# Attention with capped scores and a bilinear feed-forward on one core: a later product with the reciprocals, earlier first weights, and scores in single-pass parts

## The chip, the core and the metric

The kernel runs on one core of a Trainium2 chip. TensorE (PE in the profile) multiplies matrices into PSUM, ScalarE (ACT) evaluates functions and copies, VectorE (DVE) works element by element, GpSimd (POOL) takes what is left over, and SyncE (SP) issues nearly all the DMAs. The metric is the device time of one execution in microseconds (us). The kernel before has a median of 782.43 us over three runs.

## The reference

```python
# q, k, v: [4 batches, 12 heads, 448, 64]; w_a, w_b: [768, 1536]; w_out: [1536, 768]
scores = np.matmul(q, k.transpose(0, 1, 3, 2)) / np.sqrt(64)
scores = cap * np.tanh(scores / cap)
attn = np.exp(scores - scores.max(-1, keepdims=True))
attn = attn / (attn.sum(-1, keepdims=True) + 1e-9)
x = np.matmul(attn, v).transpose(0, 2, 1, 3).reshape(1792, 768)
out = ((x @ w_a) * (x @ w_b)) @ w_out
```

The weights arrive as 64-bit floats, so the kernel has to turn them into 32-bit ones itself; q, k and v are 32-bit.

## The kernel before

**Pairs.** The 48 heads are worked in 24 pairs: two heads of one batch, one on partitions 0 to 63, the other on 64 to 127. For a pair, `load_pair` (L191) issues four DMAs each for k and q and one for v; `prep_pair` (L205) transposes k and q on VectorE (L210). `scores` (L213) makes the transposed scores in four blocks of 128 keys, the last of 64 (448 = 3 x 128 + 64). A block is one matmul for each head, on 64 rows of the array (L223), in full fp32; a short last block takes 64 columns of weights. ScalarE applies tanh (L224) and exp (L225), and VectorE adds the exponentials of the blocks into `psum` (L229, L232, L233). `attend` (L235) multiplies the exponentials with v. Score blocks go through two PSUM buffers of two banks each (`ps_sc`); everything else takes four buffers of one bank (`ps_1`), save that from pair 12 on the product with v and the row sums of a pair take a `ps_sc` buffer together (L237).

**Normalizing.** `normalize` (L250) sums `psum` over its partitions on TensorE with a selecting matrix (L260), takes the reciprocal on VectorE (L268), writes it to DRAM (`rd`, L269) and reads it back spread over 64 partitions for each head (`den`, L273); VectorE multiplies (L274). The result is a part of x. For pairs 0 to 11 (the first 896 tokens) `split_x` (L280) splits it into a high part in fp32r, a format that TensorE takes in a single pass, and the remainder, also fp32r: `xhi` and `xlo`. For pairs 12 to 23 it goes to DRAM and is split later.

**Feed-forward.** `ffn(g)` (L365) works on one half of the tokens. Each product of two split factors is three matmuls: high by high, high by low, low by high (L377 to L379, L408 to L410). A weight tile of 128 x 768 goes through `load64` (L300, the raw 64-bit form, two buffers, SyncE), `ready_w` (L320: two steps on ScalarE, L337 and L338, three on VectorE, L339 to L341, one addition on GpSimd, L342, and a store to DRAM for the second half, L343), and `split_w` (L346).

**Order.** The main loop (L450) runs over pairs and goes through the letters of a string: P prepares the next pair, A and N attend and normalize the previous one, S and T are the first and second two score blocks, F is a share of the feed-forward:

```python
order = "PASNFTF" if pi <= NPG else "SFANPFTF"
```

Pairs 0 to 11 (NPG = 12) have no feed-forward beside them; pairs 12 to 23 run beside `ffn(0)`, and `ffn(1)` follows alone. The first `ready_w` are called at the ends of iterations 8 to 11 (L469). The written order is not the final one: a scheduler that simulates the program's time sets the order of the instructions on each engine, except for those marked with `keep_in_program_order`, as the first raw loads are (L317). On every engine work is then taken in that order, so what stands behind a waiting instruction waits too.

## Time and profile before

| | us |
|---|---|
| median of 3 runs (781.46 to 782.46) | 782.43 |
| profiled execution | 784.88 |
| its span (first to last instruction) | 783.1 |
| TensorE busy in the span | 732.6 (94%) |
| VectorE busy | 424.1 (54%) |
| ScalarE busy | 331.6 (42%) |
| GpSimd busy | 185.4 (24%) |

The span is what the profiler's rows cover; the execution's own time lies 1.8 us above it. Busy time is the union of an engine's instructions, where a matmul's end is modelled. In the rows further down, a bracket such as `[7.69 <-DMA den<-rd]` says that the engine had stood idle for 7.69 us just before, and that a DMA writing `den` from `rd` ended it.

### The profile page before, as it was taken

Reading aid. Unit: us, or ns where it says so; the run is one execution under the profiler, and the core shown is the slowest. Engines: PE = TensorE matmul, PEld = TensorE weight load, DVE = VectorE, ACT = ScalarE, POOL = GpSimd, SP = SyncE. Lnnn points to the kernel's source line nnn. Section 1 sums busy time; section 2 is a strip of 40 time slices with the busy share of each in tenths; the row PEclk is TensorE's granted clock in tenths of the full one; section 3 lists DMA queues with packets and bytes.
Section 4 is the critical chain, followed back from the end, with each engine's and each line's share of the span. In section 5 each row is a group of like instructions: output and inputs, shape, how many; then the busy total and the mean of one; then the engine's idle time right before and its main releaser. Section 6 shows DMA issues by size and latency. Waiting matters only on the chain.

```text
span 783.1 us, 10042 instructions
## 1 busy us (share of the span) xinstructions
PE 732.6 (94%) x3888; PEld 560.7 (72%) x3888; DVE 424.1 (54%) x562; ACT 331.6 (42%) x402; POOL 185.4 (24%) x102
## 2 busy tenths in 40 slices
PE   5699776997899999998999999999999999999996
PEld 1233223675587677775777787999999999999996
DVE  4576789898624876465665654733213342243222
ACT  5588587575655755354651631022232202212110
POOL 0011244364302343025340221002102201200100
PEclk9899989999899999999899999999999999999999
DMA  6455687885643664336442133542102102111002
GB/s 122 92 105 114 164 180 203 243 228 185 192 120 120 184 198 136 96 108 195 143 156 85 41 105 109 184 135 81 41 21 100 41 21 81 62 41 41 1 35 111
DMA packets 151926, 90.47 MB, mean 116 GB/s; under 512 B 114624, under 2 KB 139456, under 8 KB 151872
## 3 DMA queue, kind: packets, MB, share of 16 engines
q1 hardware_dynamic: 151872, 89.77, 40.3%
q8 instruction: 32, 0.52, 0.3%
q14 instruction: 22, 0.18, 0.1%
HBM read 67.24 MB, written 22.50 MB: 115 GB/s over the span
## 4 chain that ended last, share of the span: by engine, by line
PE 61%; DMA 17%; DVE 11%; issue 4%; SPq 3%; ACT 3%; POOL 1%; DVEq 0%; ACTq 0%; POOLq 0%
PE po L408 6%; PE po L410 6%; PE po L409 6%; PE phb L377 6%; PE phb L378 6%; PE phb L379 6%; PE pha L377 6%; PE pha L379 6%; PE pha L378 6%; DMA den<-rd 5%; PE psc L223 4%; DMA rd<-rec 4%; PE pv L245 2%; DMA xl<-xd 2%; DMA w64o<-in_moe_w_out_dram 2%
## 5 line engine op out<-in xcount | busy, mean ns | idle before, releaser
L223 PE MATMUL psc<-tq,tk 64*128 64x448 f32 (+1 forms) x384 | 97.1, 602 | 25.9 <-DVE den L274 12.3
L408 PE MATMUL po<-who,gh 128*128 128x384 f32 x336 | 114.1, 340 | 1.0 <-DVE acc L414 0.8
L409 PE MATMUL po<-wlo,gh 128*128 128x384 f32 x336 | 112.5, 335 | 0.0
L410 PE MATMUL po<-who,gl 128*128 128x384 f32 x336 | 112.5, 335 | 0.0
L377 PE MATMUL phb<-xhi,whb 128*128 128x448 f32 x288 | 108.0, 375 | 0.0
L377 PE MATMUL pha<-xhi,wha 128*128 128x448 f32 x288 | 107.6, 374 | 0.0
L378 PE MATMUL phb<-xlo,whb 128*128 128x448 f32 x288 | 106.9, 371 | 0.0
L379 PE MATMUL phb<-xhi,wlb 128*128 128x448 f32 x288 | 106.6, 370 | 0.0
L379 PE MATMUL pha<-xhi,wla 128*128 128x448 f32 x288 | 106.2, 369 | 0.0
L378 PE MATMUL pha<-xlo,wha 128*128 128x448 f32 x288 | 106.1, 369 | 0.0
L224 ACT ACTIVATE pf<-psc,capt 128x896 f32<-128x896 f32 x96 | 85.1, 909 | 44.3 <-PE psc L223 43.6
L223 PEld LDWEIGHTS psc<-tq,tk 64*128 64x128 f32 (+1 forms) x384 | 29.5, 180 | 68.6 <-issue 35.4
L225 ACT ACTIVATE pf<-pf,capt 128x1792 f32<-128x1792 f32 (+1 forms) x48 | 77.0, 1604 | 1.2
L414 DVE TENSOR_TENSOR acc<-po,acc 128x384 f32<-128x384 f32 x84 | 45.9, 554 | 48.2 <-PE po L410 48.1
L408 PEld LDWEIGHTS po<-who,gh 128*128 128x128 f32 x336 | 63.0, 188 | 8.5 <-issue 3.2
L384 DVE TENSOR_TENSOR asb<-phb,asb 128x448 f32<-128x448 f32 x48 | 29.8, 621 | 68.7 <-PE phb L379 68.6
L245 PE MATMUL pv<-pf,ldv 128*64 128x448 f32 x288 | 63.6, 563 | 2.5 <-ACT pf L225 2.5
L409 PEld LDWEIGHTS po<-wlo,gh 128*128 128x128 f32 x336 | 63.1, 188 | 0.8 <-issue 0.7
L410 PEld LDWEIGHTS po<-who,gl 128*128 128x128 f32 x336 | 63.0, 188 | 0.7 <-issue 0.7
L377 PEld LDWEIGHTS phb<-xhi,whb 128*128 128x128 f32 x288 | 55.0, 191 | 11.9 <-issue 6.1
L377 PEld LDWEIGHTS pha<-xhi,wha 128*128 128x128 f32 x288 | 54.5, 189 | 11.7 <-issue 6.1
L386 DVE TENSOR_TENSOR gl<-asb,gh 128x448 fp32r<-128x448 f32 x48 | 51.0, 1063 | 21.6 <-ACT gh L385 21.4
(73 smaller groups left out, 971.0 us busy)
## 6 DMA issues: line engine op xcount, KB each, us to landing
w64a<-in_moe_w_a_dram SPq DMA_DIRECT2D x12, 768.0 KB
w64b<-in_moe_w_b_dram SPq DMA_DIRECT2D x12, 768.0 KB
w64o<-in_moe_w_out_dram SPq DMA_DIRECT2D x12, 768.0 KB
ldk<-in_k_dram SPq DMA_DIRECT2D x96, 56.0 KB
ldq<-in_q_dram SPq DMA_DIRECT2D x96, 56.0 KB
ldv<-in_v_dram SPq DMA_DIRECT2D x24, 224.0 KB
den<-rd SPq DMA_DIRECT2D x48, 112.0 KB
out_dram<-acc SPq DMA_DIRECT2D x13, 384.0 KB
```

The source lines that it names most:

```text
L223: nc.tensor.matmul(to, tk[o, at : at + (P if n == 2 else R)], tq[o], start=True, stop=True)
L224: nc.scalar.activation(pf[:, 2 * i : 2 * i + n], psc[:, :n, :S], AF.Tanh, scale=capt[:, 1:2])
L225: nc.scalar.activation(pf, pf, AF.Exp, scale=capt[:, 0:1])
L245: nc.tensor.matmul(t[j * D : (j + 1) * D, :S], tv[:, j * (NC3 + 1) + c], p, start=(c == 0), stop=False)
L377: nc.tensor.matmul(t[:, :S], wh[:, kk], xhi[:, kk, cs], start=(kk == 0), stop=False)
L378: nc.tensor.matmul(t[:, :S], wh[:, kk], xlo[:, kk, cs], start=False, stop=False)
L379: nc.tensor.matmul(t[:, :S], wl[:, kk], xhi[:, kk, cs], start=False, stop=(kk == NK - 1))
L386: nc.vector.tensor_sub(gl[:, cs], asb[h], f32(gh[:, cs]))
L408: nc.tensor.matmul(t[:, :HALF], gh[:, cs], wh, start=(f == fs[0]), stop=False)
L409: nc.tensor.matmul(t[:, :HALF], gh[:, cs], wl, start=False, stop=False)
L410: nc.tensor.matmul(t[:, :HALF], gl[:, cs], wh, start=False, stop=(f == fs[-1]))
L414: nc.vector.tensor_add(acc[:, ti, hs], t[:, :HALF], acc[:, ti, hs])
```

## The change

Five edits:

- For pair 0 the four DMAs of q are issued by ScalarE instead of SyncE.
- `normalize` ends with the loads of `den`; the product with it, and the split or store of the result, become a step of its own, `scale`. In iterations up to 12 step M scales the pair before the one just normalized, with the product marked to keep the program's order; after iteration 12 it scales the pair just normalized, later in the iteration than before. Iteration 12 does the last of the first half at its end.
- Two raw weight tiles are loaded at the end of iteration 2, and from iteration 9 on one more is loaded before each conversion. The shifted low words go back into the raw tile, so the separate `wr` buffer is gone. `rec` has one buffer instead of two.
- For pairs from 12 on, transposed q and k are split into a high part (ScalarE, fp32r) and the remainder (VectorE), and a score block is three single-pass products instead of one in fp32. The last block of 64 keys becomes a matmul on all 128 rows, whose weights `kz` hold both heads' last keys in two corners (copied by GpSimd) and zeros elsewhere.
- In iterations 11 and 12 the transposes of the next pair move behind the second score blocks.

```diff
@@ load_pair @@
+                    eng = nc.scalar if nm == "q" and pi == 0 else nc.sync
+                    eng.dma_start(t[rows], cols.rearrange("(c p) d -> p c d", p=BLK))
@@ prep_pair @@
             nc.vector.transpose(tt, t.rearrange("p c d -> p (c d)"))
+            if pi >= NPG:
+                hi = qk.tile([P, S], F32R, tag=f"h{nm}", name=f"h{nm}_{pi}", bufs=1)
+                lo = qk.tile([P, S], F32R, tag=f"t{nm}", name=f"l{nm}_{pi}")
+                nc.scalar.copy(hi, tt)
+                nc.vector.tensor_sub(lo, tt, f32(hi))
+                tt = (hi, lo)
             stk[pi].append(tt)
+        if pi >= NPG:
+            for z, x in zip(kz, stk[pi][0]):
+                for j, o in enumerate(own):
+                    nc.gpsimd.tensor_copy(z[o, j * R : (j + 1) * R], x[o, krem[j] : krem[j] + R])
+
+    products = ((0, 0), (0, 1), (1, 0))
@@ scores, pairs from 12 on @@
+            elif n == 2:
+                for x, y in products:
+                    for j, o in enumerate(own):
+                        kk = tk[x][o, j * R + c * P : j * R + (c + 1) * P]
+                        nc.tensor.matmul(psc[:, j, :S], kk, tq[y][o], start=(x + y == 0), stop=(x == 1))
+            else:
+                for x, y in products:
+                    nc.tensor.matmul(psc[:, 0, :S], kz[x], tq[y], start=(x + y == 0), stop=(x == 1))
@@ normalize @@
-        rec = sm.tile([P, CP], F32, tag="rec", name=f"rec_{pi}")
+        rec = sm.tile([P, CP], F32, tag="rec", name=f"rec_{pi}", bufs=1)
...
-        nc.vector.tensor_mul(den, t[:, :S], den)
+        pvs[pi] = (t, den)
+
+    def scale(pi):
+        g, r = divmod(pi, NPG)
+        t, den = pvs.pop(pi)
+        tc.keep_in_program_order(nc.vector.tensor_mul(den, t[:, :S], den))
         if g == 0:
             split_x(r, den, nc.gpsimd)
@@ ready_w @@
-        lr = wp.tile([P, DM], I32, tag="wr", name=f"wl{nm}_{f}", bufs=1)
-        nc.scalar.activation(lr, lw.bitcast(U32), AF.Copy, scale=2.0**-29)
+        nc.scalar.activation(lw, lw.bitcast(U32), AF.Copy, scale=2.0**-29)
...
-        nc.gpsimd.tensor_tensor(wt, wt, lr, op=ALU.add)
+        nc.gpsimd.tensor_tensor(wt, wt, lw, op=ALU.add)
@@ main loop @@
-            order = "PASNFTF" if pi <= NPG else "SFANPFTF"
+            order = "PASMNFTF" if pi < NPG - 1 else "ASMNFTPF" if pi <= NPG else "SFANFMTPF"
...
+                elif step == "M" and (pi > NPG or pi > 1):
+                    scale(pi - (1 if pi > NPG else 2))
...
+            if pi == 2:
+                load64()
+                load64()
             if NPG - AHEAD <= pi < NPG:
+                if pi > NPG - AHEAD:
+                    load64()
                 ready_w()
...
+            if pi == NPG:
+                scale(pi - 1)
```

**Where the product stands.** VectorE, first part of the program, before: from the last addition of pair 0's exponentials to pair 1's reciprocal. A row has the line, the operation, what it writes and reads (`den_0` is pair 0's, `pf_1_0` pair 1's first exponentials), and its size.

```order
L233 TENSOR_TENSOR psum0_163<-psum0_163,pf_0_1_239 128x896
L268 RECIPROCAL rec_0_297<-sum_0_288 128x112
L229 TENSOR_TENSOR psum1_164<-pf_1_0_265 128x896
L210 STREAM_TRANSPOSE tk_3_319<-ldk_3_276 128x448
L210 STREAM_TRANSPOSE tq_3_321<-ldq_3_281 128x448
L274 TENSOR_TENSOR den_0_300<-pv_0_256,den_0_300 128x448
L232 SCALAR_TENSOR_TENSOR psum1_164<-pf_1_1_306,capt_133,psum1_164 64x448 x2
L283 CAST xhi_165<-den_0_300 128x448
L233 TENSOR_TENSOR psum1_164<-psum1_164,pf_1_1_306 128x896
L229 TENSOR_TENSOR psum0_163<-pf_2_0_332 128x896
L268 RECIPROCAL rec_1_364<-sum_1_355 128x112
```

After, from the same addition on:

```order
L257 TENSOR_TENSOR psum0_163<-psum0_163,pf_0_1_243 128x896
L290 RECIPROCAL rec_0_301<-sum_0_292 128x112
L253 TENSOR_TENSOR psum1_164<-pf_1_0_269 128x896
L213 STREAM_TRANSPOSE tk_3_320<-ldk_3_280 128x448
L213 STREAM_TRANSPOSE tq_3_322<-ldq_3_285 128x448
L256 SCALAR_TENSOR_TENSOR psum1_164<-pf_1_1_307,capt_133,psum1_164 64x448 x2
L257 TENSOR_TENSOR psum1_164<-psum1_164,pf_1_1_307 128x896
L253 TENSOR_TENSOR psum0_163<-pf_2_0_333 128x896
L301 TENSOR_TENSOR den_0_304<-pv_0_260,den_0_304 128x448
L290 RECIPROCAL rec_1_368<-sum_1_359 128x112
```

The product of pair 0 (L274, now L301) stood ahead of pair 1's second additions; now it stands behind them and behind pair 2's first addition, just ahead of pair 1's reciprocal.

**Where the first raw weights stand.** SyncE, before: the first raw tiles (`w64a_0`, `w64b_0`) and what is issued around them.

```order
L269 DMA rd7_100<-rec_7_766 8x112
L199 DMA ldk_12_945<-in_k_dram 32x14x32 x2
L273 DMA den_7_769<-rd7_100 64x448 x2
L312 DMA w64a_0_788<-in_moe_w_a_dram 128x6x256
L312 DMA w64b_0_790<-in_moe_w_b_dram 128x6x256
L199 DMA ldk_12_945<-in_k_dram 32x14x32 x2
L199 DMA ldq_12_950<-in_q_dram 32x14x32 x3
```

After:

```order
L291 DMA rd1_94<-rec_1_368 8x112
L202 DMA ldk_6_482<-in_k_dram 32x14x32 x2
L295 DMA den_1_371<-rd1_94 64x448 x2
L339 DMA w64a_0_387<-in_moe_w_a_dram 128x6x256
L339 DMA w64b_0_389<-in_moe_w_b_dram 128x6x256
L202 DMA ldk_6_482<-in_k_dram 32x14x32 x2
L202 DMA ldq_6_487<-in_q_dram 32x14x32 x2
```

They stood behind the reciprocals of pair 7 (`rd7`, `den_7`) and now stand behind those of pair 1, with the loads of pair 6 around them.

**Where the scores of a pair beside the feed-forward stand.** TensorE, before: pair 13's blocks (`psc_13_0` to `psc_13_3`) among matmuls of the feed-forward (`pha`, `phb`).

```order
L379 MATMUL pha_0_0_0_1149<-xhi_165,wla_0_0_1024 128x448
L223 MATMUL psc_13_0_1137<-tq_13_1071,tk_13_1069 128x448 x2
L377 MATMUL pha_0_0_0_1149<-xhi_165,wha_0_0_1023 128x448
L223 MATMUL psc_13_1_1141<-tq_13_1071,tk_13_1069 128x448 x2
L378 MATMUL pha_0_0_0_1149<-xlo_166,wha_0_0_1023 128x448
L379 MATMUL pha_0_0_0_1149<-xhi_165,wla_0_0_1024 128x448
...
L223 MATMUL psc_13_2_1295<-tq_13_1071,tk_13_1069 128x448 x2
...
L223 MATMUL psc_13_3_1299<-tq_13_1071,tk_13_1069 64x448 x2
```

After, its first two blocks (`hq`, `hk` are high parts, `lq`, `lk` remainders):

```order
L404 MATMUL pha_0_0_1_1213<-xlo_166,wha_0_0_1032 128x448
L244 MATMUL psc_13_0_1172<-hq_13_1148,hk_13_1142 128x448 x2
L244 MATMUL psc_13_1_1180<-hq_13_1148,hk_13_1142 128x448 x2
L405 MATMUL pha_0_0_1_1213<-xhi_165,wla_0_0_1033 128x448
...
L403 MATMUL pha_0_0_1_1213<-xhi_165,wha_0_0_1032 128x448
L403 MATMUL phb_0_0_0_1285<-xhi_165,whb_0_0_1036 128x448
L404 MATMUL phb_0_0_0_1285<-xlo_166,whb_0_0_1036 128x448
L244 MATMUL psc_13_0_1172<-lq_13_1149,hk_13_1142 128x448 x2
L244 MATMUL psc_13_0_1172<-hq_13_1148,lk_13_1143 128x448 x2
L244 MATMUL psc_13_1_1180<-lq_13_1149,hk_13_1142 128x448 x2
L244 MATMUL psc_13_1_1180<-hq_13_1148,lk_13_1143 128x448 x2
L404 MATMUL pha_0_0_1_1213<-xlo_166,wha_0_0_1032 128x448
```

The product of the high parts comes first for both blocks; the two products with a remainder follow as a group of four rows, with seven matmuls of the feed-forward in between.

## Rows read from the trace of the kernel before

**Rows 1.** Busy time by stretch: start:end, us, busy us (instructions) by engine, clock, DMA.

```profile
133.00:200.00 67.00, 58.78 (x303) 42.39 (x292) 57.11 (x63) 41.02 (x50) 33.28 (x17) 0.94 0.75 225
200.00:490.00 290.00, 285.89 (x1516) 215.68 (x1515) 172.58 (x223) 144.45 (x178) 79.01 (x41) 0.98 0.43 131
490.00:783.00 293.00, 286.07 (x1492) 270.80 (x1491) 100.26 (x147) 51.90 (x86) 40.66 (x22) 0.99 0.21 66
```

**Rows 2.** Timeline of TensorE (start, length, instruction), first score of a pair.

```profile
23.81 1.77 PE L223 MATMUL psc<-tq,tk 64*128 64x448 f32 x8
...
39.49 1.77 PE L223 MATMUL psc<-tq,tk 64*128 64x448 f32 x8
...
47.02 1.77 PE L223 MATMUL psc<-tq,tk 64*128 64x448 f32 x8
...
86.83 1.77 PE L223 MATMUL psc<-tq,tk 64*128 64x448 f32 x8
...
123.97 1.77 PE L223 MATMUL psc<-tq,tk 64*128 64x448 f32 x8
```

**Rows 3.** Timeline of VectorE, the first product with the reciprocals.

```profile
31.13 0.62 DVE L274 TENSOR_TENSOR den<-pv,den 128x448 f32<-128x448 f32 x1 [7.69 <-DMA den<-rd]
```

**Rows 4.** Timelines of VectorE, SyncE and ScalarE around the first raw weights.

```profile
87.67 0.85 DVE L268 RECIPROCAL rec<-sum 128x112 f32<-128x112 f32 x1
...
91.40 0.58 SPq L312 DMA_DIRECT2D w64a<-in_moe_w_a_dram  x1
...
96.89 0.89 ACT L337 ACTIVATE wla<-w64a 128x768 int32<-128x768 uint32 x1 [5.26 <-DMA w64a<-in_moe_w_a_dram]
```

**Rows 5.** VectorE by group (busy, mean ns), 87 to 133 us, then 39 to 62.

```profile
L232 DVE SCALAR_TENSOR_TENSOR psum<-pf,capt,psum 64x448 f32<-64x448 f32 x8 | 9.7, 1212 | 0.1
...
L232 DVE SCALAR_TENSOR_TENSOR psum<-pf,capt,psum 64x448 f32<-64x448 f32 x6 | 4.0, 674 | 1.1 <-ACT pf L225 0.9
```

**Rows 6.** Timelines of SyncE's queue and VectorE at the program's start.

```profile
2.76 2.04 SPq L199 DMA_DIRECT2D ldq<-in_q_dram  x4
...
6.70 0.65 DVE L210 STREAM_TRANSPOSE tq<-ldq 128x448 f32<-128x448 f32 x1 [1.41 <-DMA ldq<-in_q_dram]
```

**Rows 7.** ScalarE's groups for tanh and exp, the whole run (busy, mean ns).

```profile
L224 ACT ACTIVATE pf<-psc,capt 128x896 f32<-128x896 f32 x96 | 85.1, 909 | 44.3 <-PE psc L223 43.6
...
L225 ACT ACTIVATE pf<-pf,capt 128x1792 f32<-128x1792 f32 (+1 forms) x48 | 77.0, 1604 | 1.2
```

**Rows 8.** Timeline of TensorE, scores beside the feed-forward.

```profile
155.92 1.02 PE L223 MATMUL psc<-tq,tk 64*128 64x448 f32 x4
156.87 0.47 PE L377 MATMUL pha<-xhi,wha 128*128 128x448 f32 x1
157.18 0.37 PE L378 MATMUL pha<-xlo,wha 128*128 128x448 f32 x1
157.38 0.37 PE L379 MATMUL pha<-xhi,wla 128*128 128x448 f32 x1
...
166.00 1.77 PE L223 MATMUL psc<-tq,tk 64*128 64x448 f32 x8
167.70 0.47 PE L377 MATMUL phb<-xhi,whb 128*128 128x448 f32 x1
```

**Rows 9.** Timeline of TensorE's weight loads (PEld) in pair 4's scores.

```profile
47.50 0.19 PEld L223 LDWEIGHTS psc<-tq,tk 64*128 64x128 f32 x2 [0.18 <-issue]
47.88 0.19 PEld L223 LDWEIGHTS psc<-tq,tk 64*128 64x128 f32 x2 [0.18 <-issue]
```

**Rows 10.** VectorE's group for the feed-forward's remainders, the whole run.

```profile
L386 DVE TENSOR_TENSOR gl<-asb,gh 128x448 fp32r<-128x448 f32 x48 | 51.0, 1063 | 21.6 <-ACT gh L385 21.4
```

**Rows 11.** Waits of TensorE, whole run: us in total, times, longest.

```profile
PE psc L223 <- DVE den L274: 12.3, 5, 7.8
```

**Rows 12.** Timelines of TensorE and VectorE, pair 13's sums and reciprocal.

```profile
178.53 0.59 PE L260 MATMUL pv<-psum,sel 128*32 128x112 f32 x16
...
190.83 0.85 DVE L268 RECIPROCAL rec<-pv 128x112 f32<-128x112 f32 x1
```

More of the change, by code (lines that the diff above doesn't have):

```diff
@@ L184 @@
     acc = const.tile([P, NTI, DM], F32, tag="acc", name="acc")
+    kz = [const.tile([P, P], F32R, tag=f"kz{x}", name=f"kz{x}") for x in "hl"]
     own, krem = (slice(0, D), slice(D, P)), (S - R, 0)
@@ L198, in load_pair @@
                     cols = src[b, 2 * hp + j, :, h * BLK : (h + 1) * BLK]
-                    nc.sync.dma_start(t[rows], cols.rearrange("(c p) d -> p c d", p=BLK))
+                    eng = nc.scalar if nm == "q" and pi == 0 else nc.sync
+                    eng.dma_start(t[rows], cols.rearrange("(c p) d -> p c d", p=BLK))
             raw[nm, pi] = t
@@ L219, in scores @@
             psc = ps_sc.tile([P, 2, 512], F32, tag="pssc", name=f"psc_{pi}_{c}")
-            for j, o in enumerate(own):
-                at = j * R + c * P if n == 2 else krem[j]
-                to = psc[:, j, :S] if n == 2 else psc[o, 0, :S]
-                nc.tensor.matmul(to, tk[o, at : at + (P if n == 2 else R)], tq[o], start=True, stop=True)
+            if pi < NPG:
+                for j, o in enumerate(own):
+                    at = j * R + c * P if n == 2 else krem[j]
+                    to = psc[:, j, :S] if n == 2 else psc[o, 0, :S]
+                    nc.tensor.matmul(to, tk[o, at : at + (P if n == 2 else R)], tq[o], start=True, stop=True)
+            elif n == 2:
+                for x, y in products:
+                    for j, o in enumerate(own):
+                        kk = tk[x][o, j * R + c * P : j * R + (c + 1) * P]
[3 more added lines that the diff above has]
+                    nc.tensor.matmul(psc[:, 0, :S], kz[x], tq[y], start=(x + y == 0), stop=(x == 1))
             nc.scalar.activation(pf[:, 2 * i : 2 * i + n], psc[:, :n, :S], AF.Tanh, scale=capt[:, 1:2])
@@ L251, in normalize @@
         del raw["v", pi], stk[pi]
-        g, r = divmod(pi, NPG)
-        bh, hp = divmod(r, NP)
         t, ts = pvs.pop(pi)
@@ L426 @@
         nc.vector.memset(sel, 0.0)
+        for z in kz:
+            nc.vector.memset(f32(z), 0.0)
         for m in range(2):
```

## The prediction

> **What bounds the kernel now.** I read the busy times by stretch first, then TensorE's timeline, then what ended its idle time. The program has three stages: the attention of pairs 0 to 11 alone (to 133 us), pairs 12 to 23 beside the first half's feed-forward (to about 490), and the second half's feed-forward. [rows 1] shows TensorE busy 286 of 293 us in the third stage, which no edit touches, and 286 of 290 from 200 to 490: there the kernel is as long as TensorE's own work. Idle time worth having lies before 200 us. In stage one [rows 2] gives it by pairs. Each row there is the first score of a pair, of pairs 2, 3, 4, 9 and 12; 39.49 to 47.02 us is a cycle of 7.53 us with no wait in it, the bound of TensorE. From pair 2 to pair 12 ten such cycles are 75.3 us, and the rows are 100.2 apart: 24.9 us lost. It falls into: pair 2 to 3, 15.68 us (8.1 lost); pair 4 to 9, 39.8 for five cycles (2.2 lost); pair 9 to 12, 37.1 for three (14.5 lost).
>
> The first loss is VectorE standing before pair 0's product with the reciprocals until their round trip through DRAM lands [rows 3]; all its later work, the next pair's exponential sums among it, is queued behind. The third begins with ScalarE standing 5.26 us for the first raw weights, issued 5.5 us before [rows 4], with the tanh that frees score buffers queued behind; afterwards weight conversion crowds VectorE: the same additions take 1.21 us on average from 87 to 133 us, 0.67 from 39 to 62 [rows 5].
>
> **The change part by part.** All sums are against the profiled execution, span 783.1 us and 784.9 in all, 2.5 us above the median of the three runs (782.43); I take the difference over to the median.
>
> *q of pair 0 on ScalarE's queue.* SyncE issues k, then q (2.04 us), and q's transpose starts at 6.70 us [rows 6]. Issued side by side, both land about when k does, and all that SyncE issues behind moves up as much. Gain 1.8 us; no row shows a DMA issued by ScalarE, so 1 to 2.
>
> *Product one pair later, stage one.* In the order on VectorE it now stands behind the first exponential sum of the pair two later. Pair 0's reciprocals would still land at about 29 us (31.1 less the 2 us above), near the 27.7 at which VectorE now reaches the product; the 8.1 us loss shrinks to some 0.6. Later pairs have 13 us from reciprocal to product instead of none, so the 2.2 us of pairs 4 to 9 go. What is late next is TensorE itself. Gain 7.5 + 2.1 us, bounds 6 and 10.
>
> *First raw weights in the third pair.* SyncE's order shows them right behind pair 1's reciprocal round trip, and ScalarE's order has their conversion after pair 3's first exponential. By my reckoning from the rows: pair 1's reciprocal ends at 30.6 us, the load is issued 3.6 us later at 34.2 (as 87.7 + 0.85 to 91.40 before, with the same two loads between) and lands 5.5 us later, at 39.7; ScalarE is there at about 34.7. So it waits 5 us again, only earlier, and TensorE's scores with it. Then two conversions, six steps of about 0.9 us on ScalarE and three each on VectorE, stand beside attention as they stood before in pairs 9 and 10. Cost in pairs 3 to 5: 9 us. The lower bound is ScalarE's excess alone, 3.5 us (two pairs at 6.75, a 24th of the 162.1 us in [rows 7], plus 5.2, against 15.1); the upper the 10.1 us by which pairs 9 to 11 overran. In exchange pairs 9 to 12 hold two conversions where they held three: 14.5 x 2/3 = 9.7, plus about 0.5 for the first split of q and k. Gain there 4.3. Writing the shifted low words in place frees a buffer but lets the next raw load go only after GpSimd's addition, 2 us later; the wait of ScalarE on GpSimd goes for it. I take zero, plus or minus 2.
>
> Stage one in all: 1.8 + 7.5 + 2.1 + 4.3 - 9 = 6.7 us gained, between 1 and 14.
>
> *Split scores, stage two.* From [rows 8]: a feed-forward matmul of 448 columns follows the next by 0.20 us. A block of fp32 scores of two heads takes four records, 0.95 us until TensorE goes on; two blocks in one go take 1.70. So one pass over both heads costs 0.375 us, and a change of the array's form 0.2 us in all (load and drain), paid on entry and on leaving together 0.2 + what the first feed-forward matmul loses, 0.10 more. I charge 0.2 for each change. The two heads' matmuls start within the same row's merge, four records in 0.95, so they run side by side. After: three single passes at fp32r instead of two double ones. I take a feed-forward pass plus a little, 0.21 us, for two heads side by side. Per pair: 8 x 0.376 = 3.01 before; 9 x 0.21 + 3 x 0.204 = 2.50 after. Twelve pairs give 6.1 us. Changes of form, counted in the two orders: 206 and 198, since the short last block now has the feed-forward's own form, while splitting the first two blocks around feed-forward work adds one visit in ten pairs: 8 x 0.2 = 1.6. Gain 7.7. Bounds: 8 if all is hidden; if the two heads took turns, 108 passes x 0.21 = 22.7 more, a loss of 15. I stay near the first because fp32 of the same shape runs side by side.
>
> The loads of weights are hidden in the rows: within a run of scores the next load starts when a pass starts, at 47.50 and 47.88, 0.38 apart [rows 9]. The Trainium skill ("TensorE: Matmul & The Clock Gate", Part 3, "The mechanism") says that a weight load overlaps running matmuls only when its row group differs; the three products use the same two groups, so by it each load would show. This trace speaks against it.
>
> *What stage two must add.* Per pair two casts on ScalarE, two subtractions on VectorE, 1.06 us each by the like step of the feed-forward [rows 10], and four copies on GpSimd. VectorE is busy 57 of 67 us up to 200 and 173 of 290 after [rows 1], and ScalarE less, so there is room; what hides them is feed-forward work on TensorE. But q's and k's high parts have one buffer, so they are made after the previous pair's last score, and the low parts after them: 25 to 30 feed-forward matmuls (5 to 6 us) stand before the first product and only 0 to 7 before the second. Also the reciprocals of stage two still have to be back before the fourth score block, behind 40 to 64 feed-forward matmuls as before; that wait cost 12.3 us in five places, 7.8 at most [rows 11]; that one is pair 13's, whose reciprocal sat 12 us in VectorE's queue [rows 12]. I leave those and add 2 us, between 8 less and 10 more.
>
> **Sum.** 6.7 + 7.7 - 2 = 12.4 us less: 772.5 in a profile like this one, about 770 in the median.
>
> **The rivals.**
>
> *Taking turns* (slower). If fp32r matmuls of the two row groups don't overlap, the scores lose 15 us instead of gaining 7.7: 770 + 22.7 = 792.7. It turns to slower than before once a pass over both heads costs more than about 0.32 us (12.4 / 108 above 0.21). For it: no row shows fp32r at 64 rows. Against: the fp32 rows. 0.10.
>
> *Low parts late.* VectorE takes its work in order, and before pair 13's reciprocal it stood 12 us behind [rows 12]. If it is 1.3 us late on average at eleven pairs, 14 us come on top: 784. For it: up to 200 us VectorE is the busiest engine beside TensorE. Against: from 200 to 490 it is 60% busy. 0.13.
>
> *Conversions covered.* If the early pair of conversions costs ScalarE's excess alone (3.5 instead of 9), and the long wait at pair 13 goes with a lighter VectorE: 770 - 5.5 - 7 = 757.5; one of them, 763. 0.18.
>
> *The load rule.* If the skill's rule held here, a load would show in each pass.
>
> As a mechanism: a load at its full length shows after a change of form, 0.31 against 0.20 us [rows 8]; on all 108 passes 0.10 us make 10.8 us, 781. 0.04.
>
> *It doesn't do what it says:* the raw weights still come late and the wait only moves. That is inside my forecast, and is why it's not larger.
>
> **How the numbers follow.** The forecast (764 to 778) has 0.55; covered conversions 0.18; low parts late 0.13; taking turns 0.10; the load rule 0.04. A measurement tells about 0.2% (1.6 us) from no change, so same is 780.9 to 784.0. Faster: all of the forecast and of the covered case, a third of the low parts and of the load rule: 0.79. Same: 0.07. Slower: 0.14. The range, 757 to 784, leaves out taking turns and the slower half of the low parts.
>
> **What would show it.** Right: pair 3's first score near 29 us instead of 39.5; no VectorE wait over 2 us before the product in stage one; ScalarE standing some 5 us before the first conversion at 35 to 40 us, and pair 5's first score only a little before 54.5; feed-forward beginning at 125 to 128 us instead of 133.2; score passes of 0.20 to 0.22 us. Wrong: passes of 0.3 us or more (load or turns); TensorE idle before the second product of a pair, ended by the subtraction; waits for the product of more than 20 us together in stage two.

## The result

The changed kernel takes 772.15 us (median of 4 runs, 768.65 to 776.08) against 781.94 us before: a ratio of 0.9882, 95% interval 0.9851 to 0.9913. It is faster by 1.2%, the prediction said 770 and faster, and the time lies in its range. Run again in two later groups, unaltered, it took 776.21 and 776.09 us against 782.67 and 782.66 (0.9914 and 0.9913). So the gain is 6.5 to 10 us, and the profiled execution below, at 768.65, is the fastest of all its 17 runs. The experiments show that some 4 us of it, more than half of what the repeats gained, has a cause that the prediction doesn't name.

### The profile after

Busy time by stretch in the changed kernel (start:end, length, busy us and instructions of PE, PEld, DVE, ACT, POOL, then clock, DMA share, GB/s); it answers [rows 1]:

```profile
128.00:200.00 72.00, 68.68 (x357) 52.16 (x357) 61.92 (x75) 45.18 (x59) 37.49 (x30) 0.96 0.75 213
200.00:478.00 278.00, 267.15 (x1506) 214.31 (x1505) 185.67 (x234) 146.00 (x188) 91.26 (x73) 0.99 0.46 136
478.00:766.00 288.00, 282.39 (x1492) 270.22 (x1490) 100.05 (x147) 51.75 (x86) 40.81 (x22) 1.00 0.20 67
```

Two things differ. In the middle stretch TensorE, busy 286 of 290 us before, is now idle for 11 us of 278. And 1492 matmuls of the last stretch, the same number as before, take 282.4 us of TensorE where they took 286.1, though the change touches no instruction there. The granted clock, 1.00 here, was 0.99 in [rows 1], but 1.00 in both kernels over the shorter stretch compared in the section on the spacing.

Timeline of TensorE, first score of pairs 3, 4, 5, 9 and 12, as in [rows 2], and the first matmul of the feed-forward:

```profile
30.12 1.77 PE L239 MATMUL psc<-tq,tk 64*128 64x448 f32 x8
...
44.35 3.36 PE L239 MATMUL psc<-tq,tk 64*128 64x448 f32 x8 [5.33 <-ACT pf L248]
...
56.49 2.59 PE L239 MATMUL psc<-tq,tk 64*128 64x448 f32 x8
...
88.72 1.77 PE L239 MATMUL psc<-tq,tk 64*128 64x448 f32 x8
...
119.16 0.47 PE L244 MATMUL psc<-hq,hk 64*128 64x448 f32 x2 [0.91 <-ACT pf L248]
...
127.59 0.74 PE L403 MATMUL pha<-xhi,wha 128*128 128x448 f32 x1
```

Pair 3 now starts at 30.1 instead of 39.5, but pair 4 comes 14.2 us later instead of 7.53, and by pair 5 the whole lead is gone (56.5 against 54.55). Pairs 6 to 9 run without loss, and from pair 9 to pair 12 it takes 30.4 us instead of 37.1. The reason for the loss stands on the other engines, timelines of VectorE, SyncE and ScalarE, to be laid beside [rows 3] and [rows 4]:

```profile
29.92 0.62 DVE L301 TENSOR_TENSOR den<-pv,den 128x448 f32<-128x448 f32 x1 [1.41 <-DMA den<-rd]
...
36.35 0.59 SPq L339 DMA_DIRECT2D w64a<-in_moe_w_a_dram  x1
...
41.74 0.88 ACT L363 ACTIVATE w64a<-w64a 128x768 int32<-128x768 uint32 x1 [6.83 <-DMA w64a<-in_moe_w_a_dram]
```

The product waits 1.41 us instead of 7.69. The raw weights are issued at 36.35, land 5.4 us later, and ScalarE stands before them for 6.83 us, with the tanh that frees TensorE's score buffers queued behind. TensorE's clock belongs to the loss as well: while TensorE stood for its 5.33 us the granted clock fell to 0.50 (41.1 to 47.9 us, and again from 54.8 to 58.2), which is why pair 4's row above takes 3.36 us where others take 1.77.

Timeline of TensorE, a short block of split scores between matmuls of the feed-forward, to be laid beside [rows 8]:

```profile
149.85 0.37 PE L405 MATMUL phb<-xhi,wlb 128*128 128x448 f32 x1
150.15 0.47 PE L244 MATMUL psc<-hq,hk 64*128 64x448 f32 x2
150.46 0.37 PE L244 MATMUL psc<-lq,hk 64*128 64x448 f32 x2
150.66 0.37 PE L244 MATMUL psc<-hq,lk 64*128 64x448 f32 x2
150.95 0.48 PE L403 MATMUL pha<-xhi,wha 128*128 128x448 f32 x1
```

One pass over both heads (x2) costs 0.20 us, entry and exit 0.3 each with the first pass of each form at 0.31. The heads don't take turns, and no weight load shows between two passes.

### The profile page after: what moved, and what is told of

The parts are those of the page before. It is cut to its first block, busy times and chain, and to the rows that moved or that the text cites. A ratio compares the mean times of both kernels' runs of the same rounds, so it can differ in the third digit from the quotient of the medians.

```text
span 766.8 us, 10322 instructions
## 1 busy us (share of the span) xinstructions
PE 720.1 (94%) x3948; PEld 570.6 (74%) x3948; DVE 445.6 (58%) x588; ACT 338.9 (44%) x426; POOL 202.1 (26%) x150
## 4 chain that ended last, share of the span: by engine, by line
PE 42%; DMA 5%; DVE 3%; issue 1%; POOL 1%; ACT 1%; SPq 0%; POOLq 0%; ACTq 0%; DVEq 0%
PE po L435 5%; PE po L434 5%; PE po L436 4%; PE pha L405 4%; PE phb L405 4%; PE pha L403 4%; PE pha L404 4%; PE phb L404 4%; PE phb L403 4%; DMA xl<-xd 2%; PE pv L269 1%; DMA w64b<-in_moe_w_b_dram 1%; DMA w64o<-in_moe_w_out_dram 1%; DVE xlo L311 1%; PE psc L244 1%
## 5 line engine op out<-in xcount | busy, mean ns | idle before, releaser
L403 PE MATMUL pha<-xhi,wha 128*128 128x448 f32 x288 | 105.7, 367 | 0.0
L403 PE MATMUL phb<-xhi,whb 128*128 128x448 f32 x288 | 105.0, 365 | 0.0
L404 PE MATMUL phb<-xlo,whb 128*128 128x448 f32 x288 | 104.6, 363 | 0.0
L405 PE MATMUL phb<-xhi,wlb 128*128 128x448 f32 x288 | 104.3, 362 | 0.0
L248 ACT ACTIVATE pf<-psc,capt 128x896 f32<-128x896 f32 x96 | 84.3, 908 | 19.1 <-PE psc L239 9.8
L269 PE MATMUL pv<-pf,ldv 128*64 128x448 f32 x288 | 65.7, 580 | 6.6 <-ACT pf L248 5.0
L239 PE MATMUL psc<-tq,tk 64*128 64x448 f32 (+1 forms) x192 | 50.4, 632 | 17.2 <-ACT pf L248 10.3
L411 ACT CAST gh<-asb 128x448 fp32r<-128x448 f32 x48 | 27.2, 567 | 87.2 <-DVE asb L410 87.2
L386 POOL TENSOR_TENSOR wlb<-wrb,whb 128x768 fp32r<-128x768 f32 x12 | 22.2, 1847 | 155.0 <-PE pha L405 140.7
```

Source lines behind the costliest of these rows:

```text
L239: nc.tensor.matmul(to, tk[o, at : at + (P if n == 2 else R)], tq[o], start=True, stop=True)
L248: nc.scalar.activation(pf[:, 2 * i : 2 * i + n], psc[:, :n, :S], AF.Tanh, scale=capt[:, 1:2])
L269: nc.tensor.matmul(t[j * D : (j + 1) * D, :S], tv[:, j * (NC3 + 1) + c], p, start=(c == 0), stop=False)
L403: nc.tensor.matmul(t[:, :S], wh[:, kk], xhi[:, kk, cs], start=(kk == 0), stop=False)
L404: nc.tensor.matmul(t[:, :S], wh[:, kk], xlo[:, kk, cs], start=False, stop=False)
L405: nc.tensor.matmul(t[:, :S], wl[:, kk], xhi[:, kk, cs], start=False, stop=(kk == NK - 1))
```

## Experiments

Four points were open. Is the split score worth what its matmuls save? What do the early raw weights cost, and is it ScalarE's wait? What is the later product worth alone? And why is the untouched third stage 3.5 us shorter? Each kernel was timed against the kernel before on the same chip, in three groups; the kernel before has 782.67, 782.65 and 782.66 us in them, so times are also compared across groups. The table has the medians and, from each one's profile, where the first matmul of the feed-forward starts, the time from there to the first matmul of its second half (stage two), and from there to the start of the last matmul (stage three):

| kernel | us | ratio to before (95%) | first at | stage two | stage three |
|---|---|---|---|---|---|
| before | 782.7 | | 133.2 | 380.0 | 263.6 |
| changed, first profile | 772.15 | 0.9882 (0.9851 to 0.9913) | 127.6 | 373.2 | 260.0 |
| changed, again (e1) | 776.21 | 0.9914 (0.9881 to 0.9948) | 129.2 | 379.5 | 260.0 |
| changed, again (e11) | 776.09 | 0.9913 (0.9882 to 0.9944) | 130.4 | 380.1 | 260.0 |
| fp32 scores (e2) | 774.13 | 0.9892 (0.9859 to 0.9924) | 128.8 | 375.2 | 260.0 |
| late raw weights (e3) | 770.33 | 0.9829 (0.9801 to 0.9858) | 126.2 | 379.5 | 260.0 |
| spread conversions (e4) | 775.33 | 0.9889 (0.9853 to 0.9925) | 128.1 | 377.7 | 261.9 |
| before, moved (e5) | 779.0 | 0.9962 (0.9933 to 0.9992) | 134.3 | 375.9 | 260.0 |
| later product alone (e7) | 780.17 | 0.996 (0.993 to 0.999) | 126.5 | 380.9 | 263.6 |
| late raw, fp32 scores (e8) | 772.2 | 0.987 (0.9827 to 0.9913) | 122.2 | 382.6 | 260.0 |
| changed, moved (e10) | 780.75 | 0.9982 (0.9956 to 1.0008) | 129.0 | 379.3 | 263.6 |
| late raw, conversions held (e12) | 772.01 | 0.9855 (0.9822 to 0.9889) | 121.0 | 387.5 | 260.0 |

A profile is one execution, and stage two differs by up to 7 us between executions of the same kernel; stage three doesn't differ at all.

### The changed kernel again

> The changed kernel once more, unaltered, as the yardstick of this group. In its first profile a feed-forward matmul of 448 columns followed the next by 0.200 us in the third stage, in the kernel before by 0.204, at the same granted clock of 1.00. If the spacing goes with the kernel, it is 0.200 here again. If it goes with the execution, it may be 0.204 here, the time of the profiled execution then lies some 6 us above the 768.65 of the first, and the median stays at 772 plus or minus 3.

> The changed kernel unaltered, for the comparison with the moved one on the same chip: 772 to 776, spacing 0.200, third stage 260.0 us.

The spacing was 0.200 us both times. So it goes with the kernel and not with the execution, and the first profile owes its 768.65 to stage one and two alone.

### The scores

Undone alone:

```diff
 -            if pi >= NPG:
+            if False:
                 hi = qk.tile([P, S], F32R, tag=f"h{nm}", name=f"h{nm}_{pi}", bufs=1)
...
-        if pi >= NPG:
+        if False:
             for z, x in zip(kz, stk[pi][0]):
...
-            if pi < NPG:
+            if True:
                 for j, o in enumerate(own):
                     at = j * R + c * P if n == 2 else krem[j]
```

> The changed kernel with the scores beside the feed-forward in fp32 as before, and no split of q and k. By the prediction (scores worth 7.7, new waits 2) it is 5.7 us slower than the changed kernel, 778. If the waits that the splitting adds eat most of it, 772 to 775. If the two heads took turns after all, it would be faster than the changed kernel; the spacing of 0.20 us in the trace of after speaks against that.

It took 774.13 us against 776.21, which is not slower. The windows of both profiles, 200 to 480 us, first e1 (split), then e2 (fp32), columns as above:

```profile
200.00:480.00 280.00, 265.06 (x1495) 212.71 (x1495) 184.93 (x231) 146.42 (x190) 92.66 (x73) 0.99 0.45 134
...
200.00:480.00 280.00, 276.28 (x1497) 209.44 (x1496) 169.70 (x219) 140.59 (x174) 79.50 (x40) 1.00 0.46 135
```

In the same 280 us TensorE is busy 11 us less with split scores, and it does less with them: 989 matmuls of the feed-forward start there against 1035. At 480 us, with the scores of all pairs done in both, e1 is 20 such matmuls behind, 4 us. What it waits for, from 128 to 505 us (total, times, longest), first e1, then e2:

```profile
PE psc L244 <- ACT hq L217: 6.4, 5, 3.0
PE pv L269 <- ACT pf L248: 4.3, 2, 2.4
PE psc L247 <- DVE den L301: 2.7, 2, 1.4
PE psc L247 <- ACT pf L248: 2.3, 1, 2.3
...
PE psc L244 <- DVE lq L218: 1.8, 2, 1.0
...
PE psc L239 <- DVE den L301: 8.8, 3, 6.0
```

Split scores wait less for the product (2.7 us, not 8.8), but 6.4 us for q's high part, 1.8 for its remainder, and 6.6 for the tanh (L248). The longest of these in e1, timelines of ScalarE and TensorE:

```profile
288.57 0.90 ACT L363 ACTIVATE w64a<-w64a 128x768 int32<-128x768 uint32 x1 [3.13 <-DMA w64a<-in_moe_w_a_dram]
289.37 0.61 ACT L248 ACTIVATE pf<-psc,capt 128x448 f32<-128x448 f32 x1
289.89 0.55 ACT L217 CAST hq<-tq 128x448 fp32r<-128x448 f32 x1
...
290.49 0.68 PE L244 MATMUL psc<-hq,hk 64*128 64x448 f32 x4 [2.97 <-ACT hq L217]
```

The cast stands on ScalarE behind the previous pair's last tanh, and both behind a conversion that waits 3.13 us for a raw tile. The other four waits of this kind in e1 have a conversion ahead of the cast as well, which had waited 0.68 to 5.21 us for its raw tile. In the first profile, the same place, ScalarE and TensorE:

```profile
281.91 0.91 ACT L363 ACTIVATE w64a<-w64a 128x768 int32<-128x768 uint32 x1 [1.96 <-DMA w64a<-in_moe_w_a_dram]
...
283.24 0.55 ACT L217 CAST hq<-tq 128x448 fp32r<-128x448 f32 x1
...
283.84 0.67 PE L244 MATMUL psc<-hq,hk 64*128 64x448 f32 x4 [0.41 <-ACT hq L217]
```

There the raw tile is only 1.96 us late and TensorE waits 0.41 us for the cast; the total of this wait is 1.1 us against 6.4. So what the split is worth depends on how late raw tiles are.

Several of the waits cost more than their own length. Busy time by stretch, first e1, then e2:

```profile
292.15:295.56 3.41, 3.41 (x11) 3.07 (x10) 3.36 (x3) 1.43 (x3) 2.24 (x1) 0.50 0.93 237
...
188.88:199.11 10.23, 6.36 (x16) 3.31 (x16) 5.79 (x7) 5.34 (x8) 4.99 (x3) 0.50 0.62 210
```

The first stretch follows the wait of 2.97 us, the second begins within e2's longest wait, 5.98 us; in both the granted clock is 0.50, the lower of its two levels (1.2 and 2.4 GHz). In e1 it is so in three more stretches of stage two, after waits of 1.96, 2.37 and 2.28 us, and in e2 in none. Together TensorE works 12.8 us at half clock in e1's stage two and 6.4 us in e2's. A feed-forward matmul follows the next by 0.373 us there instead of 0.200, so by estimate this is about 3 us more in e1 (6.4 x (1 - 0.200 / 0.373)).

### The raw weights

Undone alone (three conversions from pair 9 on, none earlier):

```diff
-            if pi == 2:
-                load64()
-                load64()
             if NPG - AHEAD <= pi < NPG:
-                if pi > NPG - AHEAD:
-                    load64()
                 ready_w()
```

> The changed kernel with the raw weight loads where they were before (three conversions in pairs 9 to 12 again, none in pairs 3 to 5). By the prediction's terms (9 lost early, 4.3 won late) it is 4.7 us faster: 767. By the two traces (row sums of pairs 2 to 5 come 12 us late of 22.6 in the changed kernel, those of pairs 8 to 11 7 us earlier than before) 5 us faster: also 767. If the early conversions are nearly free and pairs 9 to 12 count, 776 or more.

It took 770.33, 5.9 us less than the changed kernel in the same group, the fastest kernel of the study. ScalarE still stands before the first raw tile, now in pair 9 (timeline of e3):

```profile
88.60 0.88 ACT L363 ACTIVATE w64a<-w64a 128x768 int32<-128x768 uint32 x1 [4.86 <-DMA w64a<-in_moe_w_a_dram]
```

Then the same conversions were spread out so that ScalarE doesn't stand before a raw tile early, each held back by a column that GpSimd writes in its iteration:

```diff
+        one, shift = 1.0, 2.0**-29
+        if t < 4:
+            for i, x in enumerate((one, shift)):
+                tc.keep_in_program_order(nc.gpsimd.memset(gate[t][:, i : i + 1], x))
+            one, shift = gate[t][:, 0:1], gate[t][:, 1:2]
+        nc.scalar.activation(lw, lw.bitcast(U32), AF.Copy, scale=shift)
...
-            if NPG - AHEAD <= pi < NPG:
-                if pi > NPG - AHEAD:
-                    load64()
+            if pi in (4, 6, 8, 10):
                 ready_w()
```

> The changed kernel with the first four weight conversions held to iterations 4, 6, 8 and 10 (their two ScalarE steps take their scale from a column that GpSimd writes there, marked to keep the program's order), each raw tile loaded about two pairs before. ScalarE should then stand nowhere for a raw tile in stage one. If the waits and the crowding by two conversions at once are the cost, each conversion costs ScalarE's excess of about 1 us, stage one loses 8 us rather than 23, feed-forward begins near 113 us, and the time is 757 to 760. If the conversion's work itself costs some 5 us wherever it stands, the time is 768 to 772.

Feed-forward began at 128.1 us, not 113, and the time was 775.33 (up to 3.8 us of that, 1728 x 0.0022, is a spacing of 0.202 us, since the new columns moved the weights; see below). ScalarE no longer waits for the first raw tile. What came in its place is in the timelines of SyncE, VectorE and TensorE:

```profile
36.17 0.59 SPq L340 DMA_DIRECT2D w64a<-in_moe_w_a_dram  x1
...
38.95 2.55 SPq L203 DMA_DIRECT2D ldq<-in_q_dram  x2
...
38.99 0.85 DVE L291 RECIPROCAL rec<-sum 128x112 f32<-128x112 f32 x1
...
44.01 0.58 SPq L292 DMA_DIRECT2D rd<-rec  x1
...
52.02 0.62 DVE L302 TENSOR_TENSOR den<-pv,den 128x448 f32<-128x448 f32 x1 [6.66 <-DMA den<-rd]
...
57.94 0.42 PE L283 MATMUL sum<-psum,sel 128*32 128x112 f32 x4 [5.93 <-DVE psum L258]
```

Pair 2's product waits 6.66 us for its reciprocals. They are done at 39.8, but SyncE sends them off at 44.0, behind loads whose issues, ahead of which the raw tiles went off, take up to 1.3 us each (two in 2.55, where four took 2.04 in [rows 6]), and they come back at 52. ScalarE stands as long as VectorE, since GpSimd writes the column behind the split of that product, so this kernel can't say what each wait would cost alone. It suggests that the cost of early raw tiles isn't ScalarE's wait for them alone: behind them a round trip that is meant to have a pair's time came late. The third try loads the first two at the end of iteration 7 and holds the conversions to iterations 8 to 11:

```diff
-            if pi == 2:
+            if pi == 7:
                 load64()
                 load64()
```

> The changed kernel with the first two raw weights loaded at the end of iteration 7, and the first four conversions held to iterations 8 to 11 (as in the kernel with spread conversions; the columns lie behind all other tiles, so that addresses and spacing stay those of the changed kernel). It takes ScalarE's wait for the first raw tile away without a conversion in pairs 3 to 5. If ScalarE's wait is the cost, it gains 4 us on the kernel with late raw loads (770.3): 766 or so. If the raw tiles' transfer costs as much elsewhere (the product then waits for its round trip, 6.7 us in the kernel with spread conversions), it stays at 769 to 773.

It took 772.01, within the spread of the runs of e3 (768.39 to 773.39). Here ScalarE stands before no raw tile up to 118 us (5.7 us before the columns), and the feed-forward begins at 121.0 us, 12 earlier than before. But stage two is 387.5 us, 7.5 longer than before. In the same way e8, with the feed-forward at 122.2, has a stage two of 382.6 where e2, which differs only in the raw loads, has 375.2 from 128.8 on. What stage one wins after about 126 us was given back in these two profiles. In e12 the trace shows what took it, timelines of ScalarE, VectorE and TensorE:

```profile
126.03 0.90 ACT L370 ACTIVATE w64o<-w64o 128x768 int32<-128x768 uint32 x1 [7.85 <-DMA w64o<-in_moe_w_out_dram]
...
127.74 0.56 DVE L372 TENSOR_SCALAR wto<-wto 128x768 f32<-128x768 f32 x1 [5.86 <-ACT wto L371]
128.21 0.85 DVE L292 RECIPROCAL rec<-sum 128x112 f32<-128x112 f32 x1
...
129.12 0.74 PE L410 MATMUL pha<-xhi,wha 128*128 128x448 f32 x1 [4.25 <-DVE rec L292]
```

ScalarE stands 7.85 us before a raw tile, VectorE behind ScalarE, and the reciprocal stands on VectorE behind that; the feed-forward, which had begun, waits 4.25 us until the reciprocal has read its sum. From 128.15 to 134.97 us the granted clock is then 0.50, with TensorE busy for 5.85 us: by estimate 2.7 us more. So some 7 of the 12 us that the early start won go there in this execution. In e8 the feed-forward waits 2.2 us at 140.6 for a part of x, with 6.8 us at half clock from there on. From 118 to 210 us ScalarE stands before raw tiles for 14.7 us in the kernel before, 26.1 in e12, 29.9 in e8 and 29.4 in e2; no run takes these waits away.

### The product alone

```diff
-        nc.vector.tensor_mul(den, t[:, :S], den)
+        pvs[pi] = (t, den)
+    def scale(pi):
+        g, r = divmod(pi, NPG)
+        t, den = pvs.pop(pi)
+        tc.keep_in_program_order(nc.vector.tensor_mul(den, t[:, :S], den))
...
-            order = "PASNFTF" if pi <= NPG else "SFANPFTF"
+            order = "PASMNFTF" if pi < NPG - 1 else "ASMNFTPF" if pi <= NPG else "SFANFMTPF"
```

> The kernel before with the product moved one pair later alone, and the letters of the loop's order as in the change. Feed-forward's addresses are those of before, so its spacing stays 0.204. By the prediction (7.5 + 2.1 us in stage one, nothing later) 773. If what it frees in pairs 0 to 8 is given back before the feed-forward begins (raw weights and conversions in pairs 9 to 11 end no earlier), 778 to 782.

780.17 against 782.65: 2.5 us, in the second of the two expectations. In the profile the mechanism works as predicted, pair 3 starts at 31.45 instead of 39.49, and the feed-forward begins 6.7 us earlier:

```profile
31.45 1.77 PE L223 MATMUL psc<-tq,tk 64*128 64x448 f32 x8
...
126.45 0.47 PE L380 MATMUL pha<-xhi,wha 128*128 128x448 f32 x1
```

Its profiled execution, 779.47, is 5.4 us below that of before (784.88), but that one lay above its median; the medians of 12 and 23 runs say 2.5. The lead over the kernel before is 8.0 us at pair 3 and 5.9 at pair 9 (80.97 us against 86.83), since VectorE still waits 1.3 to 1.9 us before each of the first four products.

### Scores and raw weights undone together

The two diffs of e2 and e3 in one kernel.

> The changed kernel with the raw loads where they were before and with fp32 scores throughout: of the change, the later product, the low words in place and q on ScalarE's queue are left. Its weights lie at the same place within 512 bytes as in the changed kernel. If split scores are worth nothing, as their removal alone suggests (774.1 against 776.2), it stands with the kernel with late raw loads, 768 to 771. If they are worth the 5.7 us of the prediction, 776.

772.2 against 770.3 with split scores, where e2 stood 2.1 us below e1. So split scores are worth between 2 us less and 2 us more than nothing; neither difference is clear of its interval. Beside e5 below, which is the kernel before with the same spacing of 0.200 us, e8 is 6.8 us faster. It holds the later product, the low words in place, the single buffer of `rec` and q on ScalarE's queue; the product alone gave 2.5, and how the rest divides no run shows.

### The spacing

A stretch of 216 feed-forward matmuls in stage three, its first row and the row behind its last. The kernel before, then the changed one (timelines of TensorE):

```profile
579.08 0.37 PE L377 MATMUL pha<-xhi,wha 128*128 128x448 f32 x1
...
623.15 0.33 PE L408 MATMUL po<-who,gh 128*128 128x384 f32 x1
```

```profile
565.81 0.36 PE L403 MATMUL pha<-xhi,wha 128*128 128x448 f32 x1
...
609.01 0.34 PE L434 MATMUL po<-who,gh 128*128 128x384 f32 x1
```

44.07 us and 43.20: 0.204 and 0.200 a matmul, with a granted clock of 1.00 in both. The instructions are the same ones in the same order. What differs is where their operands lie: the change adds and removes tiles ahead of the weight buffers, and the split weights start 1088 bytes higher in SBUF. So each kernel was given the other's place, by an unused tile and nothing else (1088 bytes in the kernel before, 192 in the changed one, which brings its weights to the same place within 256 bytes):

```diff
+    gap = fast.enter_context(tc.tile_pool(name="gap", bufs=1))
+    gap.tile([P, 1088 // 4], F32, tag="gap", name="gap")
     wp = fast.enter_context(tc.tile_pool(name="wp", bufs=3))
```

> The kernel before with one unused tile of 1088 bytes ahead of the weight buffers, so that the split weights and the feed-forward's products lie at the SBUF addresses that they have in the changed kernel; the order of the instructions is the same as before. If the spacing of the feed-forward's matmuls (0.204 us in the kernel before, 0.200 in the changed one, at the same granted clock) goes with the addresses, it is 0.200 here and the kernel gains 1728 x 0.004 = 6.9 us: 776 against 782.5. If it goes with something else of the change, it stays 0.204 and the time stays at 782.5.

> The changed kernel with one unused tile of 192 bytes ahead of the weight buffers, so that the split weights lie at the same place within 256 bytes as in the kernel before (64 for the weights, 192 for the data); the order of the instructions is that of the changed kernel. If the spacing goes with that place, it is 0.204 us here, the third stage is 3.5 us longer than the changed kernel's 260.0, and the time is 3.5 to 7 us above its. If the changed kernel's 0.200 has another cause, nothing changes.

The same stretch in e5, then in e10:

```profile
575.20 0.36 PE L379 MATMUL pha<-xhi,wha 128*128 128x448 f32 x1
...
618.41 0.34 PE L410 MATMUL po<-who,gh 128*128 128x384 f32 x1
```

```profile
574.28 0.37 PE L405 MATMUL pha<-xhi,wha 128*128 128x448 f32 x1
...
618.35 0.33 PE L436 MATMUL po<-who,gh 128*128 128x384 f32 x1
```

43.21 and 44.07: the spacing went with the place, both ways. In the time of e5 it shows by 3.65 us, not by the 6.9 that 4 ns on every feed-forward matmul would make; stage three alone gives 3.5. The medians make a square:

| | at before's place (0.204) | at after's place (0.200) |
|---|---|---|
| kernel before | 782.65 | 779.0 |
| changed kernel | 780.75 | 776.09 |

The place is worth 3.65 and 4.7 us, the change itself 1.9 and 2.9. The 1.9 is not clear of its interval (0.9956 to 1.0008).

Two kernels with nothing but the pattern of three matmuls on constant data measured it by itself.

> Only the feed-forward's pattern of three matmuls, on constant data and nothing else: 18 matmuls a group, three groups at each of 33 offsets of the weights (64 bytes apart, from the address of the kernel before), then three groups at each of 17 offsets of the moving data. It leaves out all of the computation. If addresses set the spacing: 0.204 us at offset 0, 0.200 at 1088 (and at 64, if the address counts within 512 bytes), about 0.202 at 1216 (as the kernel with held conversions has it). If they don't: one spacing throughout.

With the weights moved in steps of 64 bytes from before's place, the mean spacing is 0.204, 0.200, 0.203, 0.202 us, and then the same four again, up to an offset of 2048. The first matmuls at offsets 0, 64 and 128 (54 matmuls each), timeline of TensorE:

```profile
45.23 0.37 PE L38 MATMUL w<-big 128*128 128x448 f32 x1
...
56.25 0.36 PE L38 MATMUL w<-big 128*128 128x448 f32 x1
...
67.05 0.36 PE L38 MATMUL w<-big 128*128 128x448 f32 x1
```

11.02 us and 10.80. Moving the data instead gives 0.204, 0.202, 0.207, 0.200, again with a period of 256 bytes. The changed kernel's offset of 1088 is 64 within 256; e4's, 1216, is 192, with 0.202 in both.

> The same pattern of three matmuls on constant data, now with the four operands' places within 256 bytes varied one against the other in steps of 64 (256 combinations, 36 matmuls each), then both weights and both moving operands in steps of 32. It leaves out all of the computation. In the first such run the spacing repeated every 256 bytes, at 0.200 to 0.207 us. If only the two operands of one matmul count, the lowest stays near 0.200. If the weights' place against the data of the matmul that runs while they load counts, some combination comes below 0.198, and a layout by it would take up to 1728 x 0.01 = 17 us off either kernel.

The 256 combinations lie between 0.200 and 0.207 us, and in steps of 32 bytes none is lower. So 0.200 is the lowest of the layouts tried, and the changed kernel stands on it.

## Why the prediction was right, point by point

The first runs were met to 2 us and the direction too; the repeats lie 6 us above the 770, still in the range. Of its steps some held, and two errors of opposite sign hid each other, so that the number is in part luck.

**q on ScalarE's queue: mis-sized.** The term was 1.8 us; the first score starts at 6.87 instead of 7.40 (7.00 and 7.52 in the repeats). That is 0.5 us at most. Side by side both land later than k alone did: k's transpose moves from 4.64 to 5.65 us, and q's follows at 6.22.

**Product later: right mechanism, too large a size.** The wait of 7.69 us became 1.41; the cycle of pair 2 is 7.53 us, without loss; pairs 6 to 9 run at 7.53 as well. The forecast of pair 3 near 29 us met 30.1. But the term was 9.6 us, all of it won by pair 9. Alone the product had 5.9 us there, brought the feed-forward 6.7 us forward in the profile, and took 2.5 us off the median.

**Raw weights: right mechanism, mis-sized.** Forecast: issue at 34.2, landing at 39.7, ScalarE standing 5 us, 9 us lost in pairs 3 to 5 and 4.3 won in pairs 9 to 12. Found: 36.35, 41.7, 6.83 us; 13.4 lost in pairs 3 to 5 (36.0 us for three cycles, from 30.12 to pair 6 at 66.12, less 22.6) and 6.7 won. The 13.4 lies above the upper bound of 10.1; by estimate 3.2 of it is the half clock (6.95 us of work in the two stretches named above), which the sum has no term for. Pair 5, forecast a little before 54.5 us, came at 56.49. The balance, 4.7 us lost by forecast, is 5.9 by e3. That this edit makes the kernel slower was in the sum, and undoing it gives the best kernel.

**Scores: passes right, net wrong.** A pass of two heads was put at 0.21 us and is 0.20; the rivals that the heads take turns, or that each weight load shows, are out. Here one line of the Trainium skill ("TensorE: Matmul & The Clock Gate", Part 3, "The mechanism"), by which a weight load overlaps running matmuls only when its row group differs, disagrees with the trace: passes on the same two row groups, each with weights of its own, follow each other by 0.20 us, as feed-forward matmuls do. Stage two less TensorE's waits in it is 363.2 us in e2 (375.2 - 12.0) and 358.9 in e1 (379.5 - 20.6), a fall of 4.3; without the 3 us that half clock cost e1 more, TensorE's own work fell by some 7.3, near the 7.7 forecast. The step that failed is "*What stage two must add*": 2 us were put there, with low parts late as a rival of 14. Found were 8.6 us of waits (20.6 against 12.0) and the 3 us of clock behind them. The largest pieces in e1 were not VectorE's low part (1.8 us) but ScalarE's high part and tanh (6.4 and 6.6), the high part each time behind a conversion that had waited for a raw tile. So 5.7 us of gain became nothing, within 2 us by the medians.

**Low words in place: the zero was not tested alone.** The wait of ScalarE on GpSimd went as forecast: in stage two, 44.9 us in the kernel before and 15.5 in e1. But its waits for raw tiles rose from 14.7 us to 59.4 in e1 and 67.8 in e2, and they are 14.0 with the product moved alone. So the late raw tiles on which the split scores wait are in the kernels with the low words in place and not in those without (q on ScalarE's queue and the single `rec` buffer divide the kernels in the same way). The prediction named a reason, a raw load that goes only after GpSimd's addition, and put it at zero, plus or minus 2.

**Missing: the spacing.** The prediction says of the third stage that no edit touches it. No edit touches its instructions; but moving tiles changed the place of its operands, worth 3.5 us in stage three and, with stage two, 3.65 to 4.7 in the medians. No term, no rival and no row asked for it, although the two stages that are "as long as TensorE's own work" are the ones where 4 ns on each of 1728 matmuls count. The granted clock has no term either.

The sum as it should have read, against the medians of the repeats (6.5 us): the change itself 2 to 3, the place about 4. The first four runs, with 9.8, are at the upper end, and stage two's luck with raw tiles (373 us in that profile against 380 in the repeats) fits the difference: TensorE idles 14.9 us there, 20.7 and 22.6 in the repeats.

## What to carry to other kernels

Where a stage is as long as one engine's work, idle time that a faster operation leaves there has to be looked for at the operation's new inputs: name the engine that makes them and what is ahead of them in its queue, above all a wait for a large transfer. A longer wait of TensorE is to be priced with the stretch at half clock that may follow it. When tiles are added or removed, compare the spacing of matmuls that the change doesn't touch before giving the difference to the change; an unused tile that puts the old place back separates the two in one run. And a conversion placed early by a scheduler waits wherever its data lands, so moving a load alone moves the wait.

## What was not expected of the hardware

The spacing of back-to-back fp32r matmuls of 448 columns on 128 rows depends on where weights and data lie in SBUF, within 256 bytes: 0.200 to 0.207 us over 256 combinations, at full granted clock, with patterns that repeat to 1 ns (197, 202 and 201 ns in turn in the changed kernel; 200, 209, 196, 204 and 211 in the one before, a cycle of five that doesn't follow the three operands). Why, no run shows. The product matmuls of 384 columns show nothing of it: 0.1735 us before and 0.1734 after.
